# Message passing on a random graph: a different hand-out of first work units (one or two single tiles per bucket, groups of 24, batches of 6) and 160 instead of 140 one-step chunks

## The chip, the core and the metric

One NeuronCore of one Trainium2 chip runs the kernel. The metric is the device time of one launch in microseconds (us), lower is better. Three runs of the kernel before gave 9139.07, 9145.55 and 9146.39 us; the median is 9145.55.

## The reference

A graph has N = 12500 nodes with D = 64 features each and E = 800000 edges with 16 attributes. Each edge makes a message from its two end nodes and its attributes, messages are summed at the destination node, and a second small product gives the output:

```python
m_in = concatenate([x[src], x[dst], e_attr], axis=-1)     # E x 144
msg = silu(m_in @ w_msg)                                   # E x 64
agg = segment_sum(msg, dst, N)                             # N x 64
return silu(concatenate([x, agg], axis=-1) @ w_upd)
```

The inputs are drawn by `setup_inputs(seed=0)`: after `np.random.seed(seed)` come, in this order, `randn(N, 64)` for x, `randn(E, 16)` for e_attr, `randint(0, N, size=E)` for src and `randint(0, N, size=E)` for dst, then the weights. So src and dst are uniform random numbers, fixed by the seed.

## The kernel before

**Two jobs in one stream.** The kernel sorts the edges by destination and, while it sorts, already works on what is sorted. Destinations fall into 128 buckets of BK = 98 nodes. A *tile* is 128 edges (one on each partition); tile t holds the edges p·6250 + t for p = 0 to 127, so that there are NT = 6250 tiles.

**Sorting: steps and chunks.** A *step* (class `Step`) takes M = 8 tiles. It builds one-hot rows of the bucket numbers on ACT (`onehot`, L383 and L384), counts on PE how many earlier edges of the chunk have the same bucket (`count`, L410 to L413), takes each edge's rank out of that on DVE (`ranks`, L418), spreads each edge's 17-value record to the slot of its rank on DVE (`expand`, L431), and collects the records of each bucket with matmuls into one PSUM bank (`move`, L447). A *chunk* is what one PSUM bank collects before ACT evicts it (L451) and POOL scatters it to the buckets' lists in DRAM (`scatter`, L469). The first N8 chunks last for one step (8 tiles), the later ones for C = 12 tiles, so that three steps make two chunks.

**Slots and overflow.** A bucket has a limited number of slots in a chunk. The limit grows with the tile's place in the chunk:

```python
LIM = [k for k in (13, 17, 21, 24, 27, 30) for _ in range(2)]
```

An edge at place k whose rank in its bucket and chunk, counted from 0, reaches LIM[k] has no slot (L427 marks it). Then `place` (L464, L465) does not advance that bucket's pointer in that chunk: all its records of the chunk are put aside and noted in the table LOST. At the very end the kernel adds up how many chunks have such a loss. `with tc.If(more > 0)` (L1032) guards a recovery pass that is otherwise jumped over: for each noted chunk it loads the 12 tiles of the chunk again, ranks them as two half-steps, and moves them out once to find the lost buckets and then in rounds of LIM[0] = 13 slots each, with a scatter per round, into a second list; writes end marks behind it (`ends`, four scatters); forms a group of 64 single tiles from that list, of which the ones without records are dummies, and works it off with nothing beside it (`rest`); and runs the output update of all buckets a second time (16 times `load` and `run`, one after another). All loops in that pass are loops of the device.

**Working: units, groups and batches.** Sorted edges are taken as *units* of u whole tiles of one bucket. A *group* loads its tiles from DRAM (SP, L551), one DMA per unit, and is cut into *batches* of up to 8 tiles. For a batch POOL gathers the source rows, one indirect DMA per tile (`gather`, L629), DVE builds one-hot rows of the destinations (L634), PE transposes them (L643) and multiplies (L652), DVE adds (L658), ACT applies silu (L659), PE sums at the destinations (L678 or L680) and DVE adds to the accumulator (L693). Units have one tile first, then two, then QU = 4; FIRST says for the first two stages how many units each quarter of the buckets gives, the tiles of a group and those of a batch. Each unit needs its own accumulator add and its own register loads; units of four use split bf16 products in the sum.

**Order.** One *period* (function `period`) issues one step and one batch, each in four pipeline stages, in a fixed order on all queues. All of it is unrolled when the kernel is written. Which period gets which batch is decided there by a planner: `Draws` keeps 16 random fillings of the buckets (seeded generator, Poisson draws per chunk), and `step` starts a group as soon as all 16 hold its units with 6 to spare (`sure`, `holds`). Wherever no group is ready, the period has a step alone. After the last step come periods with batches alone ("tail"): the rest of the units, single tiles up to 6194 tiles in all, and a last tile of each of the 128 buckets, with the output updates (L932 to L951) between them.

Of the kernel before, what the change touches and what calls it, by code (L numbers as in the profile page):

```python
# [21 lines left out]
MAGIC = 12582912.0  # L22
M = 8
C = 12
N8 = 140
LIM = [k for k in (13, 17, 21, 24, 27, 30) for _ in range(2)]
S = LIM[-1]
S8 = LIM[M - 1]
# [2 lines left out]
BT = 8  # L31
# [1 line left out]
GT = NBG * BT  # L33
QU = 4

FIRST = [(1, 48, BT, (1, 0, 1, 0)), (2, 24, 6, (3, 3, 2, 2))]
DUM = GT
NL = {1: 16, 2: 8, QU: 8}
ZB = M // 2
# [7 lines left out]
def mpnn_kernel(tc, x, e_attr, src, dst, w_msg, w_upd, out):  # L47
# [4 lines left out]
    assert E % P == 0 and NB <= NBK and NT >= C  # L52
    K8 = min(N8, NT // (2 * M))
    NCH = K8 + (NT - K8 * M + C - 1) // C
# [16 lines left out]
    with es:  # L71
# [64 lines left out]
        done0 = cp.tile([NBK, 1], F32, name="done0")  # L136
        capm = cp.tile([NBK, 2 + len(FIRST)], F32, name="capm")

# [7 lines left out]
        stages = []  # L146
        for i, (u, gt, bt, give) in enumerate(FIRST):
            cap = capm[:, 2 + i:3 + i]
# [1002 lines left out]
```

## Time and profile before

| | before |
|---|---|
| median of three runs | 9145.55 us |
| time of the profiled execution | 9133.99 us |
| its span, first to last instruction | 9132.2 us |
| granted TensorE clock, mean | 0.966 |
| busy PE / DVE / POOL / ACT | 8125.5 / 8140.8 / 6771.0 / 5100.7 us |
| steps (L384) | 782 |
| batches (L634) | 818 |
| tiles gathered (L629) | 6322 |

The profile has, for each line of the kernel and each engine, how often an instruction ran, how long it was busy, how long its engine had been idle just before it, and what ended most of that. L384 runs once per step and L634 once per batch, so the times between their starts are the lengths of the periods. Times within a trace count from the first instruction.

### The profile page before, as it was taken

The page shows a single profiled execution, that of the slowest core. Times are in us where ns is not written, and L with a number is a line of the kernel's source. Part 1 is how long each engine was busy: PE and PEld are TensorE (multiplying, and loading weights), DVE is VectorE, ACT ScalarE, POOL GpSimd, SP SyncE. Part 2 cuts the span into 40 slices and gives each one's busy share as a digit, 9 for nine tenths or more (in the row PEclk, how much of TensorE's full clock was granted, in tenths as well). Part 3 has the DMA queues.
Part 4 walks back from the last instruction along what each step waited for, and adds up shares of the span by engine and source line. Part 5 has one row for each costly group of instructions (what it writes and reads, how often), then busy time and mean ns, then how long its engine had stood idle before and what let it go on. Part 6 is the DMA issues. An engine that isn't in the chain of part 4 may idle for free. (4 is left out here: it accounts for less than half of the span.)

```text
span 9132.2 us, 146484 instructions
## 1 busy us (share of the span) xinstructions
PE 8125.5 (89%) x44080; PEld 5898.7 (65%) x44842; DVE 8140.8 (89%) x17569; ACT 5100.7 (56%) x12609; POOL 6771.0 (74%) x6915
## 2 busy tenths in 40 slices
PE   8999999988888888898889898898888888888677
PEld 5677776666666666666666666666666666666676
DVE  7899999999999999999999999999999999998332
ACT  6566665555555555555555555555555555555222
POOL 1677777777777777777777777777777777777776
PEclk9999999999999999999999999999999999999666
DMA  2222222222222222222222222222222222222323
GB/s 66 55 60 62 61 60 56 50 56 50 55 54 50 55 51 55 49 56 51 55 50 54 56 51 50 54 55 50 56 51 54 50 55 55 51 54 48 58 48 50
DMA packets 650600, 492.47 MB, mean 54 GB/s; under 512 B 482887, under 2 KB 519303, under 8 KB 649799
## 3 DMA queue, kind: packets, MB, share of 16 engines
q0 software_dynamic: 238976, 349.72, 16.9%
q1 hardware_dynamic: 408119, 132.58, 6.9%
q8 instruction: 360, 5.90, 0.3%
q14 instruction: 441, 3.61, 0.1%
q10 hardware_dynamic: 2704, 0.66, 0.1%
HBM read 330.05 MB, written 152.30 MB: 53 GB/s over the span
## 5 line engine op out<-in xcount | busy, mean ns | idle before, releaser
L629 POOL DMA_INDIRECT g<-A_d,sidx x6322 | 6186.0, 978 | 1953.4 <-issue 1557.3
L447 PE MATMUL pl<-X,hf 128*128 128x223 f32 (+5 forms) x12512 | 4093.2, 478 | 0.0
L447 PEld LDWEIGHTS pl<-X,hf 128*128 128x128 f32 x12512 | 2303.0, 191 | 1263.5 <-issue 912.4
L431 DVE TENSOR_TENSOR X<-cb,rec 128x442 f32<-128x442 f32 (+5 forms) x3128 | 2647.3, 909 | 27.1
L383 ACT ACTIVATE hf<-iof,shi 128x128 f32<-128x128 f32 x6256 | 1909.4, 389 | 1056.7 <-PE pl L447 1053.2
L652 PEld LDWEIGHTS pre<-w,qt 114*128 114x128 f32 x10496 | 1289.8, 195 | 322.3 <-issue 298.5
L652 PE MATMUL pre<-w,qt 114*128 114x64 f32 x10496 | 1265.2, 275 | 44.3 <-DVE msg L658 39.9
L659 ACT ACTIVATE msg<-msg 128x512 f32<-128x512 f32 (+1 forms) x818 | 501.8, 613 | 1270.3 <-DVE msg L658 1265.5
L418 DVE TENSOR_REDUCE rank<-z 128x8 f32<-128x1024 f32 x782 | 949.6, 1214 | 66.5 <-PE z L413 64.6
L658 DVE TENSOR_TENSOR msg<-pre,g 128x512 f32<-128x512 f32 (+1 forms) x818 | 546.2, 668 | 485.7 <-DMA g<-A_d,sidx 285.5
L646 ACT ACTIVATE qt<-tq 114x1024 f32<-114x1024 f32 (+1 forms) x818 | 800.8, 979 | 312.2 <-PE tq L643 308.9
L411 PE MATMUL z<-G,onesb 128*128 128x384 bf16 x1564 | 515.8, 330 | 467.3 <-DVE G L392 416.4
L451 ACT ACTIVATE blk<-pl 128x512 f32<-128x512 f32 (+1 forms) x568 | 325.2, 573 | 1074.9 <-PE pl L447 1034.6
L667 DVE TENSOR_TENSOR msg<-msg 128x512 f32<-128x512 f32 x1312 | 903.6, 689 | 22.9
L384 ACT ACTIVATE hf<-hf,ones 128x1024 f32<-128x1024 f32 x782 | 899.1, 1150 | 25.4
L643 PE MATMUL tq<-ident,q 128*114 128x128 f32 x6322 | 887.1, 286 | 14.2 <-ACT nodes L188 12.8
L643 PEld LDWEIGHTS tq<-ident,q 128*114 128x114 f32 x6322 | 781.9, 142 | 139.8 <-ACT nodes L188 20.5
L678 PE MATMUL ag<-msg,q 128*98 128x192 bf16 x5248 | 580.0, 253 | 307.9 <-DVE rb L575 118.2
L469 POOL DMA_INDIRECT st<-blk,ptrs x567 | 566.7, 999 | 333.4 <-issue 147.8
L634 DVE TENSOR_TENSOR q<-cb,lo 128x784 f32<-128x784 f32 (+1 forms) x818 | 768.5, 939 | 0.7
L678 PEld LDWEIGHTS <-q 128*98 128x98 bf16 x5248 | 497.1, 126 | 396.6 <-issue 338.1
L411 PEld LDWEIGHTS <-onesb 128*128 128x128 bf16 x1564 | 152.7, 98 | 384.6 <-DVE G L392 281.1
(145 smaller groups left out, 6768.0 us busy)
## 6 DMA issues: line engine op xcount, KB each, us to landing
g<-A_d,sidx POOLq DMA_INDIRECT x6322
ea<-in_e_attr SPq DMA_DIRECT2D x260, 192.0 KB
rt<-st SPq DMA_DIRECT2D x1312, 34.0 KB
st<-blk,ptrs POOLq DMA_INDIRECT x567
rt<-st SPq DMA_DIRECT2D x434, 8.5 KB
nodes<-in_x SPq DMA_DIRECT2D x62, 98.0 KB
rt<-st SPq DMA_DIRECT2D x320, 17.0 KB
A_d<-nodes SPq DMA_DIRECT2D x32, 98.0 KB
```

Source lines behind the costliest of these rows:

```text
L383: nc.scalar.activation(c.hf[:, k, :], iof, AF.Square, bias=c.hi[:, k:k + 1])
L384: nc.scalar.activation(c.hf, c.hf, AF.Relu, bias=ones, scale=-1.0)
L418: nc.vector.tensor_reduce(out=c.rank, in_=c.z, axis=AX.X, op=OP.max)
L431: nc.vector.tensor_tensor(out=c.x[:, k:k + 2, 2:2 + n * R].rearrange("p k (s c) -> p k s c", c=R), in0=hit[:, k:k + 2, 0:n, None].to_broad ...
L447: nc.tensor.matmul(pl[:, 0:w], c.hf[:, k, :], c.x[:, k, 0:w], start=False, stop=(n == c.size - 1))
L629: nc.gpsimd.indirect_dma_start(out=t.g[:, i, :], out_offset=None, in_=A_d, in_offset=bass.IndirectOffsetOnAxis(ap=t.grp.sidx[:, k:k + 1], ...
L634: nc.vector.tensor_tensor(out=t.q[:, 0:n, 0:BK], in0=ioB[:, None, 0:BK].to_broadcast([P, n, BK]), in1=t.grp.lo[:, i0:i0 + n, None].to_broa ...
L643: nc.tensor.transpose(t.tq[0:KQ, j * P:(j + 1) * P], t.q[:, j, :], ident)
L646: nc.scalar.activation(t.qt[:, 0:w], t.tq[0:KQ, 0:w], AF.Copy)
L652: nc.tensor.matmul(t.pre[:, i * D:(i + 1) * D], t.qt[:, i * P:(i + 1) * P], w, start=True, stop=True)
L667: nc.vector.tensor_tensor(out=t.msg[:, k + 1, :], in0=t.msg[:, k, :], in1=up[:, k, :, 1], op=OP.subtract)
L678: nc.tensor.matmul(t.ag[0:BK, u * w:(u + 1) * w].rearrange("p (k d) -> p k d", d=D), q[:, i, :], m[:, :, i * D:(i + 1) * D], start=(k == 0 ...
```

## The change

Two edits of constants, with the same code around them:

```diff
-N8 = 140
+N8 = 160
...
-FIRST = [(1, 48, BT, (1, 0, 1, 0)), (2, 24, 6, (3, 3, 2, 2))]
+FIRST = [(1, 24, 6, (2, 1, 2, 1)), (2, 24, 6, (3, 3, 2, 2))]
```

The first edit makes the first 160 steps, not 140, end a chunk each. The chunks of 12 tiles begin at tile 1280 and not at tile 1120. The second edit changes the stage of single tiles: the buckets of quarters 0 and 2 give two single tiles each and those of quarters 1 and 3 give one (192 tiles; before, quarters 0 and 2 gave one and the others none, 64 tiles), in groups of 24 tiles (before up to 48) and batches of 6 (before 8). The stage of units of two tiles that follows is as before.

## The prediction

> **What bounds the kernel now.** First the page's busy times and slices.
>
> ```profile
> PE 8125.5 (89%) x44080; PEld 5898.7 (65%) x44842; DVE 8140.8 (89%) x17569; ACT 5100.7 (56%) x12609; POOL 6771.0 (74%) x6915
> ...
> PE   8999999988888888898889898898888888888677
> DVE  7899999999999999999999999999999999998332
> POOL 1677777777777777777777777777777777777776
> ```
>
> PE and DVE are level at 89%, POOL has little to do at the start and most to do in the tail, where DVE drops. So there are three phases with limits of their own. L384 runs once a step, so its starts measure the periods: the instructions of that line, asked for in five windows.
>
> ```profile
> L384 ACT ACTIVATE hf<-hf,ones x24: 1147/1148/1151, 20.7 to 214.1; 128x1024 f32<-128x1024 f32 x24
> L384 ACT ACTIVATE hf<-hf,ones x27: 1147/1148/1151, 20.7 to 241.6; 128x1024 f32<-128x1024 f32 x27
> L384 ACT ACTIVATE hf<-hf,ones x101: 1147/1149/1152, 369.0 to 1260.9; 128x1024 f32<-128x1024 f32 x101
> L384 ACT ACTIVATE hf<-hf,ones x636: 1147/1149/1162, 1315.5 to 8405.9; 128x1024 f32<-128x1024 f32 x159
> L384 ACT ACTIVATE hf<-hf,ones x782: 1147/1149/1162, 20.7 to 8405.9; 128x1024 f32<-128x1024 f32 x196
> ```
>
> The columns are count, shortest/median/longest in ns, first and last start. Steps 40 to 140 (one-step chunks beside batches of 6) are (1260.9 − 369.0)/100 = 8.92 us apart. Steps 146 to 781 (12-tile chunks beside batches of 8) are 7090.4/635 = 11.17 apart. The busy times of these stretches and of the tail:
>
> ```profile
> core 0: us, PE busy (x) PEld busy (x) DVE busy (x) ACT busy (x) POOL busy (x), PEclk, DMA share, GB/s
> 369.00:1260.90 891.90, 882.95 (x5240) 681.67 (x5341) 844.68 (x2231) 573.65 (x1433) 676.38 (x703) 1.00 0.27 61
> 1315.40:8405.90 7090.50, 6349.22 (x34135) 4479.57 (x34768) 6693.42 (x13836) 4089.62 (x10160) 5416.62 (x5494) 0.99 0.23 53
> 8405.90:9132.20 726.30, 530.73 (x3047) 493.24 (x3045) 264.72 (x677) 177.04 (x351) 526.81 (x556) 0.65 0.31 52
> ```
>
> In the first stretch PE is busy 99%, in the second DVE 94%. In the tail POOL has the turn:
>
> ```profile
> L629 POOL DMA_INDIRECT g<-A_d,sidx x375: 940/944/1315, 8630.1 to 9097.4; - x188
> ```
>
> 375 gathers start in 467.3 us, 1.25 us apart, so a batch of 8 takes 10.0 us whatever stands beside it. Per period, POOL's instructions come to 7 × 1.25 = 8.75 of 8.92 us in the first stretch and to (8 + 2/3) × 1.25 = 10.8 of 11.17 in the second: POOL is never far from being the limit either.
>
> **The change, part by part.** What is issued is fixed when the kernel is written, so I worked the planner's rule through for both sets of constants; the same working gives the old kernel's 782 steps, 818 batches and 568 chunks. It starts the first group in period 18 instead of 20 and gives the first batch in period 23 instead of 26. Periods without a batch after that: five (34 to 38) before, four (159, 160, 161, 165) after. Steps go from 782 to 783, because 6250 − 1280 = 4970 tiles need ten empty ones to fill 12-tile chunks (six before). Chunks go from 568 to 575. Beside steps, batches of four-tile units go from 636 to 617, and 32 batches of six single tiles take the place of 8 of eight. After the last step come 73 periods instead of 70, since fewer tiles fit beside steps. Gathers stay at 6322.
>
> *Start.* Steps 23 to 25 had no batch; the 24th step begins at 214.1 and the 27th at 241.6. Part of that was a wait, read from the timeline:
>
> ```profile
> 207.03 29.12 SPq L551 DMA_DIRECT2D rt<-st  x48
> 237.93 0.21 DVE L512 CAST sidx<-rt 128x64 int32<-128x64 f32 x1 [5.01 <-DMA rt<-st]
> 238.42 0.97 POOL L629 DMA_INDIRECT g<-A_d,sidx  x1 [12.63 <-DVE sidx L512]
> ```
>
> 48 single-tile loads take SP 29.1 us, 0.61 each, and DVE sat 5 us for them, with all behind L512 in its queue. 24 loads take 14.6 us over two or three periods; I leave 2 us of wait. So the first batch comes at period 23, at 216.
>
> *One-step chunks.* Periods 23 to 158 are 136 periods with one chunk and six tiles, 136 × 8.92 = 1213. In 32 of them the tiles are single, which adds three accumulator adds, register loads on PE and DVE, and six loads on SP a period. PE's 99% has no room, so I add 0.3 us each, 10 in all (bounds 0 and 1.0 each). SP's loads hide: 24 × 0.61 = 14.6 of some 36 us for four periods. The seven more scatters lie inside the 8.92. Step 159 then starts at 1439.
>
> *The boundary.* Periods 159 to 165: four without a batch, at (27.5 − 5.0)/3 = 7.5 each, as steps 23 to 25 less their wait, and three with six tiles at 9: 57. Step 166 starts at 1496, and step 782 at 1496 + 616 × 11.17 = 8377. Before, the last step started at 8405.9, so 29 us are won.
>
> *Tail.* Three more periods at 10.0 us lose 30. So what the schedule says is: no change within the 20 or 30 us of these estimates.
>
> **What the data says.** The one-step chunks also move the later chunks: they now start at tiles 1280, 1292, ... instead of 1120, 1132, .... The slots are few, so I counted the reference's own dst (seed 0; floor(dst/98), tile t of edges p·6250 + t) chunk by chunk against LIM. With 140, no bucket goes over its limit in any of the 568 chunks. With 160, one does: chunk 270, tiles 2600 to 2611, bucket 86.
>
> ```
> place in the chunk     0  1  2  3  4  5  6  7  8  9 10 11
> edges of bucket 86     4  5  8 10 13 19 22 22 24 28 30 31   (so far)
> slots                 13 13 17 17 21 21 24 24 27 27 30 30
> ```
>
> At places 9 and 11 one edge each has no slot. The chunks of before cut the same stretch at 2596 and 2608 and hold at most 25 of this bucket. So all 31 records are put aside, `more` is 1, and the branch that was jumped over is taken. Its cost, all of it behind the tail and with nothing beside it:
>
> ```profile
> L629 POOL DMA_INDIRECT g<-A_d,sidx x6322 | 6186.0, 978 | 1953.4 <-issue 1557.3
> L447 PE MATMUL pl<-X,hf 128*128 128x223 f32 (+5 forms) x12512 | 4093.2, 478 | 0.0
> L431 DVE TENSOR_TENSOR X<-cb,rec 128x442 f32<-128x442 f32 (+5 forms) x3128 | 2647.3, 909 | 27.1
> L451 ACT ACTIVATE blk<-pl 128x512 f32<-128x512 f32 (+1 forms) x568 | 325.2, 573 | 1074.9 <-PE pl L447 1034.6
> L469 POOL DMA_INDIRECT st<-blk,ptrs x567 | 566.7, 999 | 333.4 <-issue 147.8
> ...
> L383 ACT ACTIVATE hf<-iof,shi x6256: 384/388/413, 18.2 to 8405.4; 128x128 f32<-128x128 f32 x196
> L451 ACT ACTIVATE blk<-pl x568: 489/597/599, 50.4 to 8434.2; 128x512 f32<-128x512 f32 x143, 128x410 f32<-128x410 f32 x47
> ...
> L1032 SPq EVENT_SEMAPHORE  x9: 17/17/17, 9129.9 to 9130.5; - x9
> L1032 SPq COMPARE_BRANCH  x1: 54/54/54, 9126.7 to 9126.7; - x1
> ...
> 8708.22 8.90 SPq L551 DMA_DIRECT2D rt<-st  x16
> 9096.49 0.15 DVE L1002 SCALAR_TENSOR_TENSOR wl<-ptrg,ub 128x1 f32<-128x1 int32 x1
> 9097.82 0.14 DVE L1026 TENSOR_TENSOR lgi<-lg,f 1x1 int32<-1x1 f32 x1
> 9110.30 0.69 DVE L944 TENSOR_TENSOR xu<-z,xu 98x512 f32<-98x512 f32 x1 [6.35 <-PE z L942]
> 9111.02 0.63 ACT L946 ACTIVATE xu<-xu 98x512 f32<-98x512 f32 x1 [2.90 <-DVE xu L944]
> 9113.59 0.92 PE L938 MATMUL z<-ident,ACC 98*128 98x98 f32 x4 [0.78 <-DVE ACC L685]
> 9120.50 0.92 PE L938 MATMUL z<-ident,ACC 98*128 98x98 f32 x4 [0.78 <-DVE ACC L685]
> 8896.44 2.42 DMA g<-A_d,sidx
> ```
>
> These are groups of the page, lines by first and last start, pieces of the timeline, and one of the chain of waits (a gather's landing, 2.42).
>
> 1. *Loop ends and jumps.* SP jumps over the pass at 9126.7 and does its next thing at 9129.9, 3.2 us later. From 9130.5 to the end of the span, 1.7 us, the engines meet. A device loop does both: 4.9 us. I count nine (the empty loop skipped, into and out of the chunk's loop, four for the rounds, two for the last group): 44. Bounds 0 (the branch itself is 54 ns) and 72 (8 each).
> 2. *Small vectors.* The chain from L1002 to L1026 is eight small operations in 1.5 us, 0.19 each; some 45 of that kind: 9 (4 to 20).
> 3. *Loading the window again* and preparing it: a landing of 2.4 us and a dozen small operations: 7 (4 to 15).
> 4. *Two half-steps and the first move.* No row shows a step by itself. From the first L383 (18.2) to the first L451 (50.4) a step went through all stages in 32 us, other work between; 16 L383 alone are 6. I take 30, near the row of a whole step (22 to 46).
> 5. *Rounds.* 31 records at 13 a round: three. Each has six L431, 5.5 us, the last four L447 behind them, 1.9, L451 0.6, L469 1.0 and pointers 1.5: 10.5, so 32 (24 to 45).
> 6. *End marks.* Four scatters at 1.25: 5 (5 to 14).
> 7. *The group of 64.* Forming 3, 64 loads at 8.90/16 = 0.556: 36, landing 2.4, 64 gathers at 1.25: 80, and the last batch behind them some 9: 130 (125 to 150).
> 8. *Second update.* 16 times L944 0.69, L946 0.63, out-DMA and load on SP's one queue, 0.65, and the landing of 196 KB. No row gives that landing; the nearest, a gather's 2.4, is a sixth of the size, so I take 3.4, and with semaphores 6.0 a time: 96. Bounds 67 (4.2 for PE's chain alone) and 160 (10 each, the tail's own spacing).
>
> Sum 353; low ends 251, high ends 522.
>
> At term 8 the Trainium skill has a price (DMA: Bandwidth & Descriptors, "Anatomy of one DMA — SWDGE (gpsimd) path"): about 2.0 us and the bytes over 436 GB/s, an estimate of 2.5 us for 196 KB, with which the sum would be 14 us less; for a gather's 32 KB it gives 2.1, and the row has 2.42. At term 1 it speaks for less too (Runtime: NRT & Kernel Launch, "Instruction fetch mechanics"): only a jump out of the two loaded pages of instructions has to fetch, so the round loop's three jumps back would save their 3.2 us, about 10 in the sum; no row here shows a short jump.
>
> The schedule's +1 (−29 and +30) with 353 gives 354. On the profiled execution's 9133.99 that is 9488; the median of the runs stands 11.6 us higher, so 9500.
>
> **The rivals.**
>
> *The timed inputs are drawn otherwise, and no bucket overflows.* For it: the trace has no row that shows dst. Against it: seed 0 is what the reference draws by default, and before there is exactly no L384 beyond the 782 steps, which the count for seed 0 gives too. Then the recovery is jumped over as before: 9145.55 + 1 = 9147.
>
> *The gathers' head start is kept: faster.* POOL's gathers are level with the bound in every phase, so gathers done earlier could shorten the end itself. Place: steps 23 to 39. Price: the 29 us won by the last step, if the three added periods cost nothing (idle time of POOL in the tail, such as around 8490, where the four end-mark scatters stand between gathers, would have to shrink by as much). It decides only if nothing overflows: 9145.55 − 29 = 9117.
>
> *Single tiles make the early periods PE-bound: slower without overflow.* PE's 99% there speaks for it. At 1.0 us on 32 periods it is +22 against my sum: 9169, just over what counts.
>
> **How the numbers follow.** A change of less than 0.2%, 18 us, can't be told from none with this kernel. Overflow and recovery: 0.88. Without it: 0.06 no change, 0.04 faster, 0.02 slower. So faster 0.04, same 0.06, slower 0.90. The recovery's bounds on 9145.55 go from 9145.55 + 251 − 29 = 9368 to 9145.55 + 522 + 22 = 9690; that holds it about 9 times in 10 when it runs, 0.8 in all, so the range stays there.
>
> **What would show it.** Right: L384 785 times (783 and two half-steps), L629 6386 times, L932 32 times, rows of lines beyond 1040, and a last slice in which PE, DVE and POOL are nearly idle by turns; step 782 starting near 8377 and the tail's last batch near 9090. Wrong: L384 783 times and the span near 9130. Of the steps before, the weakest are terms 1, 4 and 8, for which no row has the same thing; and for the schedule, periods of single tiles above 9.3 us.

## The result, and the profile after

The change made the kernel slower: 9479.08 us (four runs, 9474.07 to 9483.44) against 9142.36 us, a ratio of 1.0369 with a 95% interval of 1.0354 to 1.0385. The profiled execution took 9474.07 us, its span is 9472.3. Lines of the page after, answering to those of before: busy times, slices, two groups, and two rows of the DMA issues.

```profile
PE 8376.6 (88%) x44942; PEld 6130.0 (65%) x45706; DVE 8192.7 (86%) x17979; ACT 5137.7 (54%) x12683; POOL 6846.2 (72%) x6993
...
PE   8999999999998999999898899998999999977764
DVE  7999999999999999999999999999999999963331
POOL 2777776777777777777777777777777777777742
...
L629 POOL DMA_INDIRECT g<-A_d,sidx x6386 | 6246.1, 978 | 2047.0 <-issue 1488.9
L384 ACT ACTIVATE hf<-hf,ones 128x1024 f32<-128x1024 f32 x785 | 902.3, 1149 | 25.5
...
rt<-st SPq DMA_DIRECT2D x690, 8.5 KB
...
xu<-XU_d SPq DMA_DIRECT2D x32, 196.0 KB
```

L384 ran 785 times: 783 steps and the two half-steps of one recovered chunk. L629 has 64 gathers more than 6322, and the output update loads its input 32 times instead of 16. The last slice has every engine idle most of the time (PE's digit is 4, DVE's 1). That is the recovery pass.

The schedule in front of it, by the starts of L384 in three windows after (steps 0 to 23, 23 to 159 and 166 to 782):

```profile
L384 ACT ACTIVATE hf<-hf,ones x24: 1147/1148/1150, 18.9 to 213.8; 128x1024 f32<-128x1024 f32 x24
L384 ACT ACTIVATE hf<-hf,ones x137: 1147/1149/1155, 213.8 to 1440.1; 128x1024 f32<-128x1024 f32 x137
L384 ACT ACTIVATE hf<-hf,ones x617: 1147/1149/1168, 1501.0 to 8381.4; 128x1024 f32<-128x1024 f32 x155
```

The store of the last nodes (L951), in the kernel before:

```profile
L951 SPq DMA_DIRECT2D out<-xu x1: 792/792/792, 9125.9 to 9125.9; - x1
```

and after:

```profile
L951 SPq DMA_DIRECT2D out<-xu x2: 426/430/433, 9130.1 to 9469.3; - x2
```

Before, it is issued at 9125.9 and ends the work; after, it comes at 9130.1, 4 us later, and a second time at 9469.3. So all but 4 us of the loss stand behind the first store. The busy times of that stretch, cut where its work changes:

```profile
core 0: us, PE busy (x) PEld busy (x) DVE busy (x) ACT busy (x) POOL busy (x), PEclk, DMA share, GB/s
9130.50:9145.70 15.20, 1.40 (x5) 1.11 (x6) 7.26 (x37) 0.32 (x2) 0.00 (x0) 0.50 0.11 23
9145.70:9168.80 23.10, 14.76 (x34) 7.04 (x35) 11.19 (x19) 8.44 (x22) 0.00 (x0) 0.64 0.00 0
9168.80:9216.40 47.60, 29.39 (x75) 16.48 (x74) 21.20 (x51) 1.80 (x4) 2.94 (x3) 0.86 0.04 16
9216.40:9272.20 55.80, 1.36 (x8) 0.89 (x8) 3.52 (x27) 0.62 (x2) 3.86 (x5) 0.51 0.16 30
9272.20:9389.40 117.20, 63.91 (x320) 61.96 (x320) 27.32 (x82) 14.43 (x22) 60.56 (x64) 0.53 0.79 18
9389.40:9472.30 82.90, 47.01 (x192) 36.78 (x192) 11.06 (x16) 18.05 (x32) 0.00 (x0) 0.50 0.30 78
```

In order: into the pass and the window loaded again; two half-steps and the first move; three rounds; end marks and 64 loads; 64 gathers and eight batches; the second update. Together 341.8 us, in which PE, DVE, ACT and POOL are each idle for a third of every part or more.

### The profile page after: what moved, and what is told of

It reads as the page before. It is cut to its first block, busy times and chain, and to the rows that moved or that the text cites. A ratio compares the mean times of both kernels' runs of the same rounds, so it can differ in the third digit from the quotient of the medians.

```text
span 9472.3 us, 150584 instructions
## 1 busy us (share of the span) xinstructions
PE 8376.6 (88%) x44942; PEld 6130.0 (65%) x45706; DVE 8192.7 (86%) x17979; ACT 5137.7 (54%) x12683; POOL 6846.2 (72%) x6993
## 5 line engine op out<-in xcount | busy, mean ns | idle before, releaser
L629 POOL DMA_INDIRECT g<-A_d,sidx x6386 | 6246.1, 978 | 2047.0 <-issue 1488.9
L447 PE MATMUL pl<-X,hf 128*128 128x223 f32 (+4 forms) x12616 | 4151.5, 480 | 5.6 <-DVE X L431 5.6
L447 PEld LDWEIGHTS pl<-X,hf 128*128 128x128 f32 x12616 | 2345.8, 193 | 1287.5 <-issue 907.6
L431 DVE TENSOR_TENSOR X<-cb,rec 128x442 f32<-128x442 f32 (+2 forms) x3154 | 2661.0, 906 | 27.4
L652 PEld LDWEIGHTS pre<-w,qt 114*128 114x128 f32 x10112 | 1260.2, 197 | 390.1 <-issue 366.4
L652 PE MATMUL pre<-w,qt 114*128 114x64 f32 x10112 | 1239.4, 277 | 112.5 <-DVE msg L658 112.5
L643 PE MATMUL tq<-ident,q 128*114 128x128 f32 x6386 | 923.9, 292 | 64.2 <-DVE q L634 49.1
L643 PEld LDWEIGHTS tq<-ident,q 128*114 128x114 f32 x6386 | 815.3, 146 | 196.9 <-issue 67.1
L384 ACT ACTIVATE hf<-hf,ones 128x1024 f32<-128x1024 f32 x785 | 902.3, 1149 | 25.5
L667 DVE TENSOR_TENSOR msg<-msg 128x512 f32<-128x512 f32 x1264 | 870.4, 689 | 22.0
L652 PE MATMUL pre<-BW,qt 114*128 (+1 forms) x2660 | 396.1, 311 | 144.1 <-DVE msg L658 135.0
```

The lines of the kernel that those rows point to most:

```text
L384: nc.scalar.activation(c.hf, c.hf, AF.Relu, bias=ones, scale=-1.0)
L431: nc.vector.tensor_tensor(out=c.x[:, k:k + 2, 2:2 + n * R].rearrange("p k (s c) -> p k s c", c=R), in0=hit[:, k:k + 2, 0:n, None].to_broad ...
L447: nc.tensor.matmul(pl[:, 0:w], c.hf[:, k, :], c.x[:, k, 0:w], start=False, stop=(n == c.size - 1))
L629: nc.gpsimd.indirect_dma_start(out=t.g[:, i, :], out_offset=None, in_=A_d, in_offset=bass.IndirectOffsetOnAxis(ap=t.grp.sidx[:, k:k + 1], ...
L643: nc.tensor.transpose(t.tq[0:KQ, j * P:(j + 1) * P], t.q[:, j, :], ident)
L652: nc.tensor.matmul(t.pre[:, i * D:(i + 1) * D], t.qt[:, i * P:(i + 1) * P], w, start=True, stop=True)
```

## The experiments

Theory A: one bucket of one chunk has more records than slots, because the chunks are cut elsewhere, and the recovery pass is the whole loss. Theory B: the schedule costs it (one-step chunks, single-tile units). Theory C, added after the first runs: the schedule costs some 0.7%, beside the recovery. Each run is compared with the kernel before on its own chip. Two of the chips ran every kernel some 31% slower (before at 11973 and 12040 us); there, pieces of one trace are compared rather than whole times.

**Moving the cut by one chunk** (`e1_cut161`, `e1b_cut161`, `e1c_cut161`):

```diff
-N8 = 160
+N8 = 161
```

> N8 = 161 with the new FIRST: one more one-step chunk, and the 12-tile chunks begin at tile 1288, which cuts tiles 2600 to 2611 at 2608 as before; no bucket overflows in the reference's data. Theory A (the slowdown is the recovery pass that one overflowing bucket starts): the whole loss goes; 9130 to 9160 us, L384 782 times, no row of a line between 1040 and 1130. Theory B (the slowdown is in the schedule: one-step chunks and single-tile units): 9470 to 9490, as with 160.

> N8 = 161 with the new FIRST once more, since the four runs before came from a chip on which every kernel took some 31% longer and this one was 0.75% slower than before. On a chip where before takes some 9140: theory A (recovery alone) 9130 to 9160, ratio 0.998 to 1.002. Theory C (the schedule of the change itself costs some 0.7% and hid in the sum): ratio 1.005 to 1.010.

> N8 = 161 with the new FIRST a third time, now for a chip on which before takes some 9150. Theory A (the recovery pass is the whole loss): ratio 0.998 to 1.002, step 781 starts near 8375. Theory C (the schedule of the change costs by itself): ratio 1.003 or more.

On the slower chips 1.0075 (1.0047 to 1.0102) and 1.0025 (0.9993 to 1.0057); on a chip like the first ones 9127.33 us against 9140.02, 0.9987 (0.9978 to 0.9996). The first of these alone would have spoken for theory C; on another chip the difference can't be told from none, and where before takes 9140 us the sign is the other way. The steps of the third run:

```profile
L384 ACT ACTIVATE hf<-hf,ones x782: 1147/1149/1164, 20.3 to 8357.5; 128x1024 f32<-128x1024 f32 x196
```

782 steps, none for a recovery. With one one-step chunk *more* than the slow version, the loss is gone. On this chip it takes 13 us less than the kernel before, 0.1%; on the slower chips it takes no less, so a gain is not shown.

**The two edits apart** (`e2_oldfirst160`, `e3_newfirst140`, `e3b_newfirst140`), on the slower chips:

```diff
-FIRST = [(1, 24, 6, (2, 1, 2, 1)), ...     # e2: N8 = 160, old hand-out
+FIRST = [(1, 48, BT, (1, 0, 1, 0)), ...       # as in the kernel before
...
-N8 = 160                                   # e3: N8 = 140, new hand-out
+N8 = 140
```

> N8 = 160 with the old FIRST (48 single tiles in batches of 8 first). The chunk cuts are those of the changed kernel. Theory A: the loss is there in full, 9470 to 9500 us, L384 785 times. Theory B with the hand-out as the cause: back to 9130 to 9160.

> N8 = 140 with the new FIRST: no overflow, the hand-out of units alone. Theory A: within 25 us of before, 9120 to 9165; by counting periods it has 25 without a batch beside steps instead of 31 and 72 instead of 70 after the last step, which comes to some 15 us less than before, 9130. Theory B with the hand-out as the cause: over 9300.

> N8 = 140 with the new FIRST, the hand-out of units alone, no overflow. Theory A: ratio 0.997 to 1.002; by the count of periods 15 us less than before, 0.998. Theory C with the hand-out as its cause: 1.005 or more.

e2: 1.0264 (1.0223 to 1.0304), 313 us more. In its trace the pass begins with L1040 and runs to the end of the span:

```profile
L1040 DVE TENSOR_REDUCE vb<-LOST x1: 752/752/752, 11969.9 to 11969.9; 128x1 f32<-128x575 f32 x1
...
span 12316.9 us, 149635 instructions
```

That is 347 us, and 338 by the same count in the changed kernel (9134.3 to 9472.3). The absolute times expected of e2 belong to a faster chip; the loss is there, as theory A has it. e3: 1.0024 (0.9991 to 1.0057) and 0.9991 (0.9955 to 1.0028): no change that these chips can show, and no recovery.

**Fewer one-step chunks with the same cuts** (`e5_cut130_old`):

```diff
-N8 = 140                                   # the kernel before, old FIRST
+N8 = 130
```

> The kernel before with N8 = 130 alone: ten one-step chunks fewer, old FIRST. The 12-tile chunks begin at tile 1040 and so cut at 2600 and 2612 again, as with 160; the count finds the one bucket over its limit there and nowhere else. Theory A (where the chunks are cut decides, not how many one-step chunks there are): slower by 310 to 360 us, L384 785 times. Rival (more one-step chunks cost): not slower than before.

9509.92 us against 9153.75, 1.0389 (1.0371 to 1.0406), 356 us more. Steps and the start of its recovery:

```profile
L384 ACT ACTIVATE hf<-hf,ones x785: 1147/1149/1162, 20.4 to 9173.7; 128x1024 f32<-128x1024 f32 x197
...
L1040 DVE TENSOR_REDUCE vb<-LOST x1: 742/742/742, 9156.0 to 9156.0; 128x1 f32<-128x565 f32 x1
```

Ten one-step chunks fewer than before, and the loss is the same as with 20 more, within the two intervals. So it is where the chunks are cut (1040 and 1280 leave the same remainder by 12), not how many there are.

**Without the second update** (`e7_no_second_update`):

```diff
-            for t in us.values():
-                t.load()
-                t.run()
```

> The changed kernel without the second output update at the end of the recovery pass; the messages of the 31 recovered edges don't reach the output. The trace after has 4.73 us for each of 16 updates one behind the other: 78 us less than the changed kernel, 255 to 270 us over before. Rival (the updates hide behind something else, the end marks' or the group's transfers): under 30 us less.

9397.99 us against 9153.75, 1.0269 (1.0252 to 1.0286): 244 us over before (255 to 270 expected, so that forecast missed), and by the ratios 1.0% or 91 us less than the changed kernel. The two intervals leave that open by some 20 us either way, so the 78 of the forecast and the 82.9 of the stretch above both fit. The rival, under 30 us, does not: the updates are not hidden.

**A group of 8 tiles instead of 64** (`e6_small_group`), on a slower chip:

```diff
-grp = Group(1, ptr, done, done, ceil, base=base).all()
+grp = Group(1, ptr, done, done, ceil, gt, base=base).all()   # gt = 8 for the second list; batches and groups are counted by it
```

> The changed kernel, but the recovery's group has 8 tiles (one batch) instead of 64. If the group's cost is as the trace after shows it, one thing after the other, 56 loads at 0.58 us and 7 batches at 13.4 us go: 32 + 94 = 126 us less, some 9353, ratio 1.022 to 1.025. If loop ends and fetches of instructions make up most of the pass (the rival), less than 60 us go, ratio over 1.030.

1.0171 (1.0118 to 1.0224), below the 1.022 to 1.025 expected. That ratio was meant for a chip on which before takes some 9150 us; the 211 us that were to remain (337 less 126) are a ratio of 1.0175 on 12040. The changed kernel itself was not run on this chip. The pass in three parts (to the first gather, gathers to the update, update to the end), with 64 tiles on the same chip (`e4b_spread_sentinels`, below, whose filler records differ):

```profile
12122.70:12261.60 138.90, 47.66 (x122) 25.96 (x123) 43.11 (x134) 11.16 (x27) 6.77 (x7) 0.65 0.09 19
12261.60:12383.10 121.50, 65.55 (x320) 61.49 (x320) 27.09 (x82) 14.31 (x22) 60.53 (x64) 0.51 0.07 18
12383.10:12466.40 83.30, 46.99 (x192) 36.75 (x192) 11.06 (x16) 18.06 (x32) 0.00 (x0) 0.50 0.30 78
```

and with 8:

```profile
12011.40:12118.50 107.10, 48.86 (x122) 26.62 (x123) 42.97 (x134) 10.97 (x26) 6.78 (x7) 0.69 0.06 20
12118.50:12140.10 21.60, 8.53 (x40) 7.77 (x40) 3.68 (x12) 1.65 (x2) 7.61 (x8) 0.50 0.40 13
12140.10:12220.10 80.00, 47.01 (x192) 36.76 (x192) 11.07 (x16) 18.07 (x32) 0.00 (x0) 0.50 0.30 80
```

The loads lose 31.8 us (32 forecast), the batches 99.9 (94 forecast): the group is work in a row, and loop ends are not most of the pass. The filler is not likely to make this difference: in e2, which has the filler of the changed kernel and ran on the other slower chip, the batches take as long as in e4b:

```profile
12113.00:12234.00 121.00, 61.28 (x320) 57.47 (x320) 27.14 (x82) 14.43 (x22) 60.61 (x64) 0.54 0.76 18
```

**Filler records that name other rows** (`e4_spread_sentinels`, `e4b_spread_sentinels`, `e4c_spread_sentinels`). The trace after raised the question: a batch took 13.4 us in the recovery and 10 in the tail.

```diff
-nc.gpsimd.memset(sent[:, :, DE:R], (P - 1) / 256.0)
+nc.vector.tensor_scalar(out=sent[:, :, DE], in0=iof[:, 0:32], scalar1=390.0, scalar2=(P - 1) / 256.0, op0=OP.mult, op1=OP.add)
```

> The changed kernel, and the records that fill empty places name 32 different source rows far apart instead of row 0 (their messages are added nowhere, as before). In the recovery pass 63 of the 64 gathered tiles hold nothing else. Theory H (a batch there takes 13.4 us instead of 10 because all 128 partitions of all its gathers read one row, whose packets take about 1.45 us instead of 0.19): a batch goes back to 10 to 10.5 us, the DMA share there from 0.89 to under 0.4, and the time falls by 15 to 30 us. Rival (the periods there are long because PE runs at half clock and one stage waits for the other): 13 us a batch, within 5 us of the changed kernel.

> The changed kernel with filler records that name 32 rows far apart instead of row 0. Theory H (63 of 64 gathered tiles of the recovery read one row, and its packets take 1.45 us): its batches go from 13.4 us to some 10.2, the DMA share there to under 0.4, the time falls by 15 to 30 us, ratio to before 1.033 to 1.036. Rival (half clock and stages that wait for each other): 13 us a batch and a ratio of 1.036 to 1.039.

> The filler records that name 32 rows far apart, for a chip on which before takes some 9150. On the slower chips POOL waited for the gathers 1.2 us instead of 12.8 us, but PE's stalls ended the batches. Theory H: where PE does not stall, batches of 10 to 10.5 us instead of 13.4, 15 to 30 us less than the changed kernel, ratio to before 1.033 to 1.0355. Rival (the stages wait for each other at half clock whatever the gathers do): ratio 1.036 to 1.039.

On the slower chips 1.0416 (1.0375 to 1.0457) and 1.0334 (1.0299 to 1.0370), which decides nothing; the batches took 121.5 us there, as long as with one row in e2 (both above), so there the rows of the filler do not decide. On a chip like the first, 9448.44 us against 9140.02, 1.0336 (1.0320 to 1.0351), by the ratios 30 us less than the changed kernel. The gathers of the recovery, by start and by what POOL waited for, in the changed kernel:

```profile
L629 POOL DMA_INDIRECT g<-A_d,sidx x64: 942/946/976, 9272.2 to 9368.1; - x64
  DMA g<-A_d,sidx: 23.0, 34
```

and with the other rows, with the busy row of its stretch:

```profile
L629 POOL DMA_INDIRECT g<-A_d,sidx x64: 940/945/973, 9274.1 to 9352.9; - x64
  DMA g<-A_d,sidx: 2.1, 7
...
9274.10:9363.90 89.80, 61.66 (x320) 59.85 (x320) 27.30 (x82) 14.54 (x22) 60.46 (x64) 0.54 0.10 24
```

From the first to the last gather 78.8 us instead of 95.9, from the first gather to the second update 89.8 instead of 117.2, the DMA share 0.10 instead of 0.79 for the same bytes (24 GB/s for 89.8 us and 18 for 117.2 are both 2.1 to 2.2 MB). PE's granted clock is 0.54 here and 0.53 there, so the rival of the half clock falls. That one row was the cause of the longer batches is shown on this chip.

## Why the prediction was right

The forecast was 354 us more, 9500; measured are 337 more, 9479. The step that decided, the count of the reference's own destinations, held: exactly one chunk was recovered (785 and not 787 rows of L384), and the kernels with the cut at 2600 and 2612 pay it (e2, e5) while those with the cut elsewhere do not (e1c, e3). That the recovery's sum came within 12 us is in part luck, since its terms were off by up to 28.

*Schedule.* Forecast: first batch at 216, step 159 at 1439, step 166 at 1496, step 782 at 8377, +1 us in sum. Measured: first batch at 213.2, step 159 at 1440.1, step 166 at 1501.0, step 782 at 8381.4 and the end of the ordinary work 4 us later than before. So the last step starts 24.5 us earlier and what follows it is 28.7 longer (8381.4 to 9130.1, before 8405.9 to 9125.9). Single tiles did not hold up the early periods: 1226.3 us from step 23 to 159, where 1223 were forecast. The rival of a kept head start would have had its case with 161, which needs one step less: e1c starts its last step at 8357.5. But its 13 us stand on one chip alone, and what makes them is not shown.

*Terms 1 to 3.* Too dear. In the first stretch fall terms 2 and 3 and two of the nine loop ends (the empty loop, the way into the chunk's loop): some 26 us forecast, 15.2 measured. The other ends lie in the stretches that follow. The starts of a round, in pieces of the timeline after (scatter of one round, last operation of it, first of the next, its scatter):

```profile
9179.98 1.00 POOL L469 DMA_INDIRECT st<-blk,ptrv  x1 [63.98 <-ACT blk L451]
9182.84 0.16 DVE L1118 TENSOR_TENSOR ptrv<-left,ptrv 128x1 int32<-128x1 f32 x1 [6.21 <-DMA st<-blk,ptrv]
9182.98 0.15 DVE L1120 TENSOR_SCALAR rs<-rs 128x1 f32<-128x1 f32 x1
9184.21 0.23 DVE L424 TENSOR_SCALAR left<-rank,rs 128x8 f32<-128x8 f32 x1 [1.07 <-PEq L1113]
9185.75 9.83 PE L447 MATMUL pl<-X,hf 128*128 128x223 f32 x24 [0.90 <-DVE X L431]
9196.49 0.98 POOL L469 DMA_INDIRECT st<-blk,ptrv  x1 [15.51 <-ACTq L1113]
```

From L1120's end to the next round 1.1 us pass, where I had 4.9. I had applied the far jump's row to the loop's short one. The Trainium skill, which I had weighed and not used, says that a taken jump has to fetch when its target lies outside the two loaded pages (Runtime: NRT & Kernel Launch, "Instruction fetch mechanics"). The trace agrees as far as times go: 1.1 us here, 3.2 at the far jump of before. What was loaded, no run shows.

*Term 5.* A round is 16.5 us (9179.98 to 9196.49), where I had 10.5 and a loop end of 4.9. PE's matmuls are the missing part: 24 of them take 9.8 us one behind the other, with DVE's spreading beside them, where I had the last four alone, 1.9 us. And the pointer waits for the scatter's landing (L1118, 1.9 us after the scatter's issue ends). Two errors that nearly cancel, the rounds too cheap and their loop ends too dear: the stretch is 47.6 against 32 + 20.

*Term 4* 23.1 for 30. *Terms 6 and 7 up to the gathers* 55.8 for 46 and two loop ends (10). That this agrees is luck: the two ends took 2.9 and 0.8 us, and the end marks were too cheap. They start 3.5 us apart, each behind the landing of the one before, where I had the 1.25 of gathers:

```profile
9226.69 0.96 POOL L961 DMA_INDIRECT st<-sent,pe  x1 [2.54 <-DMA st<-sent,pe]
9230.19 0.96 POOL L961 DMA_INDIRECT st<-sent,pe  x1 [2.53 <-DMA st<-sent,pe]
```

*Gathers and batches:* 117.2 for 89. The step that failed is the pace of 1.25 us from the tail: these gathers read one row. With other rows the stretch took 89.8.

*Term 8.* 80 us from the first load (9389.4) to the last store (9469.3) for 96. One update of the trace after:

```profile
9399.90 0.33 SPq L949 DMA_DIRECT2D out<-xu  x1
9400.33 0.46 SPq L932 DMA_DIRECT2D xu<-XU_d  x1
9403.23 0.69 DVE L944 TENSOR_TENSOR xu<-z,xu 98x512 f32<-98x512 f32 x1 [4.01 <-DMA xu<-XU_d]
9403.95 0.63 ACT L946 ACTIVATE xu<-xu 98x512 f32<-98x512 f32 x1 [3.24 <-DVE xu L944]
```

The load's issue ends at 9400.79 and DVE goes on at 9403.23: a landing of 2.44 us, where I took 3.4. The Trainium skill's price for this size (DMA: Bandwidth & Descriptors, "Anatomy of one DMA — SWDGE (gpsimd) path"), an estimate of 2.5 us from its fit, was the better one. The fit is for DMAs that GpSimd issues and this one SP issues; the trace agrees all the same, 2.44.

In sum 341.8 of 353: the gathers 28 too cheap, the first stretch, the half-steps, the rounds and the update 4 to 16 too dear each. The forecast of a loss of this size rests on the count and on work in a row; its nearness to the measured time does not show that each price was right.

## What to carry to other kernels

A kernel with fixed slots and a slow path for overflow has a time that hangs on the data: a constant that moves only a boundary can put one bucket one record over. Count the slots against the data for each such constant before looking at the schedule; here 140 and 161 are free of it and 130 and 160 are not, at some 340 us a time. A slow path that is taken once costs what its fixed sizes cost (64 tiles for 31 records, a second update of everything), so size it for the small case.

## What the runs showed of the hardware

Gathers of 128 rows that all name one row of DRAM (63 of the 64) held the DMA engines busy for 0.79 of the time at 18 GB/s, and POOL issued one in 95.9/63 = 1.52 us; with 32 rows far apart the share was 0.10 at 24 GB/s, and one was issued in 78.8/63 = 1.25. On the chip where this was tried, filler indices are better spread; on the slower chips the batches took 121 us either way (e2, e4b).

On two chips every kernel took some 31% longer. The same kernel on both kinds of chip (`e1c_cut161`, then `e1b_cut161`), its busy times and the waits of PE's weight loads for nothing that the profile shows (us in total, times, longest):

```profile
PE 8290.8 (91%) x45058; PEld 5988.3 (66%) x45058; DVE 8102.7 (89%) x17735; ACT 5086.8 (56%) x12592; POOL 6760.9 (74%) x6922
PEld pl L447 <- issue: 899.9, 4640, 0.4
...
PE 9224.9 (76%) x44296; PEld 6580.4 (54%) x45058; DVE 8167.0 (68%) x17735; ACT 5062.4 (42%) x12592; POOL 6680.2 (55%) x6922
PEld pl L447 <- issue: 1277.4, 4895, 5.1
```

DVE, ACT and POOL are busy for about as long in both. PE is busy 934 us more, at a granted clock of 0.834 instead of 0.954 (a matmul of L447 takes 505 ns instead of 479). That is a third of the 2967 us by which the span is longer. The rest is time in which PE is idle; in this group of loads the longest gap is 5.1 us instead of 0.4. What makes the gaps was not tried and stays open.
